# Attention weights turned by VectorE and regrouped by transfers, and fp32 scores with heads side by side, from the second batch on

## The chip, the cores and the metric

The kernel runs on one NeuronCore of a Trainium2 chip. The metric is the device time of one execution in microseconds, lower is better. The engines of the core that matter here are TensorE (PE in the profile, with its weight loads as PEld), VectorE (DVE), ScalarE (ACT), GpSimd (POOL), and SyncE (SP), which issues every DMA.

## What is computed

Block-causal attention over 8 batches of 8 heads, 576 tokens, 64 channels per head, followed by a gated MLP with a spatial gate. All inputs are float32.

```python
# attention, block = 64
scores = scale * np.matmul(q, k.transpose(0, 1, 3, 2))
scores = np.where(block_i >= block_j, scores, -1000000000.0)
attn = np.exp(scores - np.max(scores, axis=-1, keepdims=True))
attn = attn / (np.sum(attn, axis=-1, keepdims=True) + 1e-09)
x = heads_side_by_side(np.matmul(attn, v))          # (8, 576, 512)
# gated MLP
h = np.maximum(x @ w_in, 0.0)                       # (8, 576, 1024)
u, v = (h[..., :512], h[..., 512:])
v_n = (v - mean(v)) / np.sqrt(var(v) + 1e-06)
v_s = np.einsum('ts,bsd->btd', w_spatial, v_n) + b_spatial[None, :, None]
return (u * v_s) @ w_out
```

## The kernel before, in words

Batches are numbered 0 to 7 here. Heads go in pairs, four pairs a batch (`NPAIR`), the first head of a pair in partitions 0 to 63, the second in 64 to 127. A pair has nine score tiles (`TILES`): for each head the query tiles t = 0 to 3 with 128, 256, 384 and 512 keys, and one tile for query block 8 of both heads, with all 576 keys. The main loop at L639 walks over all tiles of all pairs, one tile a step.

A step calls `scores` (L276). PE forms the tile, DVE copies it from PSUM with the mask and takes the row minimum of the scaled negative (L298, L319), ACT takes the exponential with the row sum (L325), DVE forms the reciprocal (L331, L334), and POOL multiplies it in (L338). In batch 0 the products take the float32 operands (L293). From batch 1 on the operands are split into an upper and a lower part in the rounded type fp32r: ACT rounds (L222), DVE and POOL subtract (L225), ten transfers a pair stack the parts so that two products over 128 rows give all cross terms (L235 to L243, L296, L297; three for the tile of block 8, L315).

Some steps later `transposes` (L353) turns the tile with PE through an identity, in 128 by 128 pieces (L366 to L388), into PSUM, and ACT or DVE copies the result to SBUF (L369, L376, L383). `av_lo` (L408) and `av_hi` (L422) multiply with the values in float32, the two heads in the two column halves of the array, and `x_evac` splits the output into two parts (L404 and L405). The last 64 tokens are copied once more, both parts side by side, by POOL into `xs` (L445).

`moe` (L451) returns 29 groups of matmuls for a batch: five `v_group` (the normalised half; 12 matmuls of 512 columns, the one for the last 64 tokens 8), eight `u_group`, eight `sp_group` (the spatial gate, 14 matmuls of 288 columns), eight `out_group` (12 of 288). All use fp32r parts in three products. The groups of batch b run during the steps of batch b + 1, 29 groups for 36 steps, so that one group stands between about any two attention tiles. A group's PSUM bank comes from a pool of two (`ps_m`, tag `m`). A v group's chain runs on ACT (relu, L473), DVE (statistics L489 and L490, small ops L493 to L505), ACT (L491, L492), and DVE (L509, L516, L517). The output tile `o` has two buffers, and each goes out by a DMA on SP (L588).

The order on each engine is fixed when the program is built: a scheduler places the instructions of the written order, with some freedom where nothing depends.

## Time and profile before

| what | value |
|---|---|
| runs | 761.75, 763.27, 765.53 us (median 763.27) |
| span of the profiled execution, first to last instruction | 760.0 us |
| the profiled execution's own time beside its span | the page gives the span alone; the median of the runs is 3.3 us above it |
| PE busy | 750.3 us, 5284 matmuls |
| DVE, ACT, POOL busy | 486.7, 453.3, 316.7 us |
| DMA moved | 96.37 MB, 52% busy share of the 16 engines in batches 1 to 7 |
| granted TensorE clock | 1.00 in every stretch asked for |

A matmul's record has a start and a modelled end, and neighbours overlap in the pipeline. So the time that a matmul takes from PE is read from start to start, or from the chain of waits, which gives each piece the time by which it moves the chain on, and not from its recorded length. A float32 product appears as two records (two passes), an fp32r product as one. Times within a batch are given from the first v group of one batch to the same place of the next.

### The profile page before, as it was taken

The page shows a single profiled execution, that of the slowest core. Times are in us where ns is not written, and L with a number is a line of the kernel's source. Part 1 is how long each engine was busy: PE and PEld are TensorE (multiplying, and loading weights), DVE is VectorE, ACT ScalarE, POOL GpSimd, SP SyncE. Part 2 cuts the span into 40 slices and gives each one's busy share as a digit, 9 for nine tenths or more (in the row PEclk, how much of TensorE's full clock was granted, in tenths as well). Part 3 has the DMA queues.
Part 4 walks back from the last instruction along what each step waited for, and adds up shares of the span by engine and source line. Part 5 has one row for each costly group of instructions (what it writes and reads, how often), then busy time and mean ns, then how long its engine had stood idle before and what let it go on. Part 6 is the DMA issues. An engine that isn't in the chain of part 4 may idle for free.

```text
span 760.0 us, 16034 instructions
## 1 busy us (share of the span) xinstructions
PE 750.3 (99%) x5284; PEld 648.9 (85%) x5284; DVE 486.7 (64%) x1744; ACT 453.3 (60%) x1236; POOL 316.7 (42%) x478
## 2 busy tenths in 40 slices
PE   8999899999999999999999999999999999999998
PEld 5567798988888889988888889988889988888898
DVE  6997985668545785448755487555865568543641
ACT  6786766655665656566656566655666556654232
POOL 4785775423444325443344334433344423423011
DMA  6477585555465445464355554456454554430001
GB/s 216 138 212 219 146 232 128 129 134 124 114 171 125 115 119 135 133 173 111 85 141 150 141 124 103 127 152 159 106 130 116 139 146 112 92 77 33 0 9 55
DMA packets 43814, 96.37 MB, mean 127 GB/s; under 512 B 6866, under 2 KB 15570, under 8 KB 43732
## 3 DMA queue, kind: packets, MB, share of 16 engines
q1 hardware_dynamic: 43732, 95.35, 48.4%
q8 instruction: 42, 0.69, 0.4%
q14 instruction: 40, 0.33, 0.1%
HBM read 38.18 MB, written 9.44 MB: 63 GB/s over the span
## 4 chain that ended last, share of the span: by engine, by line
PE 87%; DVE 7%; ACT 2%; issue 2%; DMA 1%; SPq 0%; DVEq 0%; ACTq 0%
PE mo L581 14%; PE ms L560 13%; PE mu L537 12%; PE mv L468 11%; PE avh L430 7%; PE t L375 6%; PE s L297 4%; PE s L296 4%; PE s L315 3%; PE avl L415 3%; PE t L382 2%; PE t L368 2%; PE mv L479 1%; PE avh L434 1%; DVE p L298 1%
## 5 line engine op out<-in xcount | busy, mean ns | idle before, releaser
L338 POOL TENSOR_SCALAR p<-p,ssum 128x384 f32<-128x384 f32 (+4 forms) x288 | 175.0, 615 | 252.0 <-DVE ssum L334 96.6
L325 ACT ACTIVATE p<-p,nmax 128x384 f32<-128x384 f32 (+4 forms) x288 | 168.5, 586 | 59.4 <-DVE nmax L298 38.7
L298 DVE CUSTOM_DVE_ANT_0 p<-s,mask 128x128 f32<-128x128 f32 (+3 forms) x256 | 122.7, 486 | 60.2 <-PE s L297 46.4
L537 PE MATMUL mu<-x,wi_hi 128*128 128x288 f32 x512 | 116.3, 303 | 0.5 <-DVE vr L485 0.5
L537 PEld LDWEIGHTS mu<-x,wi_hi 128*128 128x128 f32 x512 | 85.4, 188 | 2.9 <-ACT pthi L376 1.0
L468 PE MATMUL mv<-wi_hi,x 128*128 128x512 f32 x256 | 85.9, 396 | 0.0
L225 POOL TENSOR_TENSOR lo<-raw,hi 128x288 fp32r<-128x288 f32 (+1 forms) x83 | 68.3, 837 | 37.4 <-ACT hi L222 37.4
L331 DVE TENSOR_SCALAR ssum<-ssum 128x1 f32<-128x1 f32 (+1 forms) x224 | 39.1, 175 | 63.8 <-ACT p L325 63.3
L560 PE MATMUL ms<-ws_hi,vh 128*128 128x288 f32 x256 | 78.6, 307 | 0.0
L560 PE MATMUL ms<-ws_hi,vl 128*128 128x288 f32 x256 | 75.4, 294 | 0.0
L560 PE MATMUL ms<-ws_lo,vh 128*128 128x288 f32 x256 | 75.3, 294 | 0.0
L581 PE MATMUL mo<-gh,wo_hi 128*128 128x288 f32 x256 | 74.5, 314 | 0.5 <-ACT gh L568 0.5
L376 ACT COPY pthi<-t 128x384 f32<-128x384 f32 (+1 forms) x128 | 67.8, 530 | 9.9 <-PE t L375 9.1
L568 ACT CAST gh<-u 128x288 fp32r<-128x288 f32 x64 | 27.7, 433 | 75.1 <-DVE u L567 72.7
L297 PE MATMUL s<-st 128*128 128x128 f32 (+1 forms) x224 | 72.3, 323 | 0.0
L296 PE MATMUL s<-st 128*128 128x128 f32 (+1 forms) x224 | 71.5, 321 | 0.0
L375 PE MATMUL t<-ident,p 128*128 128x128 f32 x448 | 70.8, 275 | 0.4 <-POOL p L338 0.3
L537 PE MATMUL mu<-x,wi_lo 128*128 128x288 f32 x256 | 69.7, 295 | 0.0
L581 PE MATMUL mo<-gh,wo_lo 128*128 128x288 f32 x256 | 69.7, 295 | 0.0
L569 POOL TENSOR_TENSOR gl<-u,gh 128x288 fp32r<-128x288 f32 x48 | 38.7, 806 | 64.6 <-ACT gh L568 63.8
L430 PE MATMUL avh<-pthi,v 128*64 128x320 f32 x384 | 61.0, 441 | 0.4 <-DVE x L405 0.4
L375 PEld LDWEIGHTS t<-ident,p 128*128 128x128 f32 x448 | 52.3, 141 | 8.6 <-issue 3.0
(119 smaller groups left out, 1726.0 us busy)
## 6 DMA issues: line engine op xcount, KB each, us to landing
raw<-qk SPq DMA_DIRECT2D x31, 608.0 KB, 5.0
st<-lo SPq DMA_DIRECT2D x112, 144.0 KB, 3.1
st<-hi SPq DMA_DIRECT2D x56, 272.0 KB, 3.2
v<-v SPq DMA_DIRECT2D x32, 320.0 KB, 3.4
outT<-o SPq DMA_DIRECT2D x64, 144.0 KB, 2.5
st<-hi SPq DMA_DIRECT2D x56, 144.0 KB, 3.1
st<-lo SPq DMA_DIRECT2D x56, 128.0 KB, 3.3
rwi<-w_in SPq DMA_DIRECT2D x8, 512.0 KB, 4.5
```

Source lines behind the costliest of these rows:

```text
L225: (nc.vector if n < (2 if (b, pr) == (1, 0) else 1) else nc.gpsimd).tensor_tensor(out=lo[:, cs], in0=raw[:, cs], in1=hi[:, cs].bitcast(F32 ...
L296: nc.tensor.matmul(ps[:, :n], st[:, qs], st[:, Q8:Q8 + n], start=True, stop=False)
L297: nc.tensor.matmul(ps[:, :n], st[:, qs], st[:, :n], start=False, stop=True)
L298: nc.vector.tensor_tensor_reduce(out=pt[:, :n], in0=ps[:, :n], in1=mask[:, 512 - n:], scale=-0.125, scalar=BIG, op0=ALU.add, op1=ALU.min, ...
L325: nc.scalar.activation(pt[:, :n], pt[:, :n], AF.Exp, bias=mx, scale=-1.0, accum_out=ssum[:, sc:sc + 1])
L338: nc.gpsimd.tensor_scalar(out=pk[:, :nk], in0=pk[:, :nk], scalar1=ssum[:, 2 + sc - k:3 + sc - k], scalar2=1.0, op0=ALU.mult, op1=ALU.mult,)
L375: nc.tensor.transpose(bk[:, c, :], pt[:, c * P:(c + 1) * P], ident)
L430: nc.tensor.matmul(av[js, 0:320], vt[:, c, js], hi[:, j, c, :], start=(c == 0), stop=False)
L468: nc.tensor.matmul(ps, xs[k][:, j, cs], w[:, k, DH:], start=(n == 0), stop=(n == 3 * NC - 1),)
L537: nc.tensor.matmul(ps[:, :HT], w[:, k, ds], xs[k][:, j, zs], start=(n == 0), stop=(n == 3 * NC - 1),)
L560: nc.tensor.matmul(ps[:, :HT], a[:, ds], w[:, k, zs], start=(n == 0), stop=False)
L581: nc.tensor.matmul(ps[:, :HT], w[:, k, es], a[:, k, :], start=(n == 0), stop=(n == 3 * ND - 1),)
```

## The change

In batch 0 the attention stays as it was (its output columns are stored in another token order, so one copy becomes two). From batch 1 on:

- **Scores** take the float32 operands from the raw tile. The splitting (`prep_pair`, its ACT, DVE and POOL instructions and its transfers) is gone. A pair's eight tiles t = 3 to 0 are written as one run, the two heads alternating, each in its own 64 rows of the array; the tile of block 8 stands ahead of it (`scores_8`, `scores_run`).
- **Transposes** leave PE. `turn_blocks` turns the tile on DVE in 32 by 32 blocks (`nc.vector.transpose`, 13 instructions a pair, 3,200 elements a partition) into one tile `pb`, and `regroup` issues four transfers a head on SP, which gather the blocks into `ptt`. Tokens are stored in another order (`tokens`), and the inputs and the output are permuted to it on the host. The PSUM copies of the transposes on ACT and DVE are gone.
- **Outputs** of a pair are one run of 20 products (`av_pair`), placed right behind the scores of the next pair.
- **MLP**: PE's order is now fixed as written (`mm`). One group stands between the block-8 tile and the score run, and the others behind the outputs, as many as a credit in microseconds allows. The group of the last 64 tokens comes first in its batch instead of fifth. In a v group the scaling and the rounding move from DVE to ACT, the subtraction from DVE to POOL; in the last sp group of four the subtraction moves to POOL.
- Score, output and transpose banks are used as one ring of six (`RING`).

```diff
-    raw_p = ctx.enter_context(tc.tile_pool(name="raw_p", bufs=1))
-    hl_p = ctx.enter_context(tc.tile_pool(name="hl_p", bufs=1))
-    qk_p = ctx.enter_context(tc.tile_pool(name="qk_p", bufs=3))
+    raw_p = ctx.enter_context(tc.tile_pool(name="raw_p", bufs=2))
...
-    p_p = ctx.enter_context(tc.tile_pool(name="p_p", bufs=4))
+    p_p = ctx.enter_context(tc.tile_pool(name="p_p", bufs=6))
...
-    def prep_pair(b, pr):
...
+    def mm(out, lhsT, rhs, start, stop):
+        ins = nc.tensor.matmul(out, lhsT, rhs, start=start, stop=stop).ins
+        if last[0] is not None:
+            tc.add_manual_dep(
...
+    RING = [(ps_s, "s")] * 3 + [(ps_t, "t")] * 2 + [(ps_av, "av")]
...
+    def scores_8(b, pr):
...
+        for z in range(2):
+            ps = bank(f"s8_{b}_{pr}_{z}")
+            mm(ps[:, :HT], raw[:, Q8:], raw[:, z * HT:(z + 1) * HT], True, True)
...
+    def scores_run(b, pr):
...
+        for t in (3, 2, 1, 0):
+            for hd in range(2):
...
+                mm(ps[(t, hd)], raw[js, S + t * P:S + (t + 1) * P], raw[js, :n], True, True)
+        for ts in ((3,), (2,), (1, 0)):
...
+                    soft(st, t, hd, p[:, at:at + n], [ps[(t, hd)]])
...
+            normalise(st, tiles)
...
+    def turn_blocks(b, pr, t, hd):
...
+        if t == 8:
+            dims = [[XH, 8], [1, 16]]
+            nc.vector.transpose(to(P, [[P, 3], *dims]), p8[:, :384])
+            nc.vector.transpose(to(304, dims), p8[:, 384:512])
+            nc.vector.transpose(to(144, dims), p8[:, 512:640])
+            return
...
+        nc.vector.transpose(to(hd * XH + 32 * t, [[P, m], *dims] if m > 1 else dims), p[:, :m * P])
+        if t == 3:
+            nc.vector.transpose(to(hd * XH + x_at(3, 3), dims), p[:, 3 * P:])
+
+    def regroup(b, pr, hd):
...
+        for a in range(4):
+            nc.sync.dma_start(ptts[(b, pr)][:, a, xs], pb[32 * a:32 * a + 32, :, xs])
...
+    def av_pair(b, pr):
...
+        for z in range(2):
+            av = bank(f"av_{b}_{pr}_{z}")
...
+            for c in range(5):
+                for j in range(2):
...
+                    mm(
+                        to[js, :, PA - C_N[c]:], vt[:, c, js],
+                        ptt[:, 2 * z:2 * z + 2, at:at + C_N[c]], c == 0, c == 4,
+                    )
...
-            nc.vector.tensor_scalar(
-                out=vr[:m, :], in0=vr[:m, :], scalar1=st[:m, 12:13], scalar2=st[:m, 13:14],
-                op0=ALU.mult, op1=ALU.add,
+            nc.scalar.activation(
+                vr[:m, :], vr[:m, :], AF.Identity, bias=st[:m, 13:14], scale=st[:m, 12:13]
             )
...
-                nc.vector.tensor_copy(vh, vr)
-                nc.vector.tensor_tensor(
+                nc.scalar.copy(vh, vr)
+                nc.gpsimd.tensor_tensor(
...
-            (nc.vector if dc == ND - 1 else nc.gpsimd).tensor_tensor(
+            nc.gpsimd.tensor_tensor(
...
+        vs = [(G_V if c < FULL else G_VT, lambda c=c: v_group(c)) for c in (FULL, 0, 1, 2, 3)]
...
+    for g in range(NPAIR, len(pairs)):
+        b, pr = pairs[g]
+        credit += G_PAIR
...
+        scores_8(b, pr)
+        group()
+        scores_run(b, pr)
+        if g > NPAIR:
+            av_pair(*pairs[g - 1])
+            if pr == 0:
+                queue += moe(b - 1)
...
+        while group():
...
+            for f in rest[:3]:
+                f()
+            del rest[:3]
+        for f in rest:
+            f()
```

Here `C_N` is (144, 112, 80, 48, 16), `rest` holds the pair's block-8 turn, its tile turns and its two regroups, and `normalise` issues POOL's multiplication per tile, as L338 did.

Three places show what the new order is. The first is PE's stream where a batch ends and the first MLP group that needs it begins. Names are output<-weights and moving operand: `avh` and `av` are attention outputs, `mv` a v group, `x` an output of a pair, `xs` its last 64 tokens. Before:

```order
L430 MATMUL avh_3_3563<-pthi_3_3225,v_3_2815 64x320 x6
L434 MATMUL avh_3_3563<-pthi_3_3225,v_3_2815 64x192 x2
L439 MATMUL avh_3_3563<-ptc_2_3_3226,v_3_2815 64x64 x2
L296 MATMUL s_0_4_3580<-st_0_1_3183 128x256
L297 MATMUL s_0_4_3580<-st_0_1_3183 128x256
L468 MATMUL mv_0_3589<-wi_hi,x_0_2451 128x512
L468 MATMUL mv_0_3589<-wi_lo,x_0_2451 128x512
```

and now:

```order
L231 MATMUL av_3_1_1946<-ptt_3_1793,v_3_1490 64x2x80 x2
L231 MATMUL av_3_1_1946<-ptt_3_1793,v_3_1490 64x2x48 x2
L231 MATMUL av_3_1_1946<-ptt_3_1793,v_3_1490 64x2x16 x2
L231 MATMUL mv_4_1964<-wi_hi,xs_1189 128x512
L231 MATMUL mv_4_1964<-wi_lo,xs_1189 128x512
```

The first group behind the batch's last outputs was a v group that reads `x`; it is now the group of the last 64 tokens, which reads `xs`, and the scores of a whole pair stand right ahead of the outputs.

The second place is POOL's stream around the write of that `xs`. Before (`p` are tiles of attention weights, `lo` a lower part of the split):

```order
L338 TENSOR_SCALAR p_3_8_3380<-p_3_8_3380,ssum_3_8_3379 128x512
L225 TENSOR_TENSOR lo_1_3470<-raw_1_3437,hi_1_3469 128x288 x2
L338 TENSOR_SCALAR p_0_0_3420<-p_0_0_3420,ssum_0_0_3419 128x576
L225 TENSOR_TENSOR lo_1_3470<-raw_1_3437,hi_1_3469 128x128
L338 TENSOR_SCALAR p_0_1_3463<-p_0_1_3463,ssum_0_1_3462 128x128
L338 TENSOR_SCALAR p_0_2_3495<-p_0_2_3495,ssum_0_1_3462 128x256
L445 TENSOR_SCALAR xs_2452<-x_3_3399 128x128
```

and now (`p_2_0_0` and `p_2_0_1` are the tiles of the next batch's first pair, `p_96` its block-8 tile):

```order
L497 TENSOR_SCALAR p_96<-p_96,sst_0_1871 128x576
L497 TENSOR_SCALAR p_2_0_0_1896<-p_2_0_0_1896,sst_0_1871 128x512
L497 TENSOR_SCALAR p_2_0_1_1899<-p_2_0_1_1899,sst_0_1871 128x512
L497 TENSOR_SCALAR p_2_0_0_1906<-p_2_0_0_1906,sst_0_1871 128x384
L497 TENSOR_SCALAR p_2_0_1_1909<-p_2_0_1_1909,sst_0_1871 128x384
L497 TENSOR_SCALAR p_2_0_0_1916<-p_2_0_0_1916,sst_0_1871 128x256
L497 TENSOR_SCALAR p_2_0_0_1916<-p_2_0_0_1916,sst_0_1871 128x128
L497 TENSOR_SCALAR p_2_0_1_1921<-p_2_0_1_1921,sst_0_1871 128x256
L497 TENSOR_SCALAR p_2_0_1_1921<-p_2_0_1_1921,sst_0_1871 128x128
L409 TENSOR_SCALAR xs_1189<-x_3_1943 128x128
```

All nine tiles of a pair of the next batch are normalised ahead of the copy that the first MLP group reads.

The third place is DVE's stream at the statistics of the last full v group (`st_3`, of `vr_3`). Before:

```order
L517 TENSOR_TENSOR vl_2_2508<-vr_2_2483,vh_2_2507 128x512
L331 TENSOR_SCALAR ssum_1_1_2512<-ssum_1_1_2512 128x2
L334 RECIPROCAL ssum_1_1_2512<-ssum_1_1_2512 128x2
L298 ISA p_1_3_2600,nmax_1_3_2598<-s_1_3_2601,mask 128x128
L298 ISA nmax_1_3_2598 128x1
L489 BN_STATS st_3_2571<-vr_3_2570 128x6
```

and now:

```order
L396 TENSOR_TENSOR x_0_2229<-av_0_0_2218,x_0_2229 128x288
L494 RECIPROCAL sst_1_2143<-sst_1_2143 128x4
L396 TENSOR_TENSOR x_0_2229<-av_0_1_2233,x_0_2229 128x288
L563 STREAM_TRANSPOSE pb_1_2280<-p_2_1_0_2202 128x2x4x32
L563 STREAM_TRANSPOSE pb_1_2280<-p_2_1_0_2202 128x4x32
L563 STREAM_TRANSPOSE pb_1_2280<-p_2_1_1_2207 128x2x4x32
L563 STREAM_TRANSPOSE pb_1_2280<-p_2_1_1_2207 128x4x32
L639 BN_STATS st_3_2253<-vr_3_2252 128x6
```

The statistics now stand behind all thirteen block turns of the pair, the last four of which are shown.

## Prediction

> **What bounds the kernel now.** First the page's busy times and the shares of the chain of work that ended last.

> ```profile
> PE 750.3 (99%) x5284; PEld 648.9 (85%) x5284; DVE 486.7 (64%) x1744; ACT 453.3 (60%) x1236; POOL 316.7 (42%) x478
> PE 87%; DVE 7%; ACT 2%; issue 2%; DMA 1%; SPq 0%; DVEq 0%; ACTq 0%
> ```

> PE is never without a matmul, and it is most of the chain. Next the busy times by stretch, each from the same place of one batch to that of the next (columns: us, PE, PEld, DVE, ACT, POOL, clock, DMA share, GB/s).

> ```profile
> 156.44:247.84 91.40, 91.40 (x661) 80.76 (x661) 58.01 (x213) 55.68 (x153) 36.66 (x58) 1.00 0.52 131
> 430.66:522.07 91.41, 91.41 (x661) 80.77 (x661) 58.03 (x213) 55.71 (x153) 36.66 (x58) 1.00 0.53 133
> ```

> The period is 91.41 us, PE fills all of it, and DVE has 58. Seven such periods (attention of batches 1 to 7 beside the MLP of 0 to 6) are 640 of the 760.0 us; the other 120 are batch 0's attention and the last MLP, which the change leaves nearly alone. So the question is one period: what PE must do in it, and how long PE now waits in it. The chain in order of time (start, us, piece) prices PE's work:

> ```profile
> 301.81 1.57 PE mo L581 x12
> 303.38 0.23 PE s L296
> 303.61 0.23 PE s L297
> 303.84 0.33 PE t L375 x3
> 304.17 0.80 PE avl L415 x8
> 304.97 1.78 PE mo L581 x12
> 306.75 0.79 PE s L315 x6
> 307.54 0.44 PE t L375 x4
> ...
> 313.09 1.77 PE avh L430 x12
> 314.86 0.32 PE avh L434 x4
> 315.18 0.26 PE avh L439 x4
> 315.44 1.79 PE ms L560 x12
> 317.24 0.13 PE ms L564
> 317.37 0.14 PE ms L565
> ...
> 352.71 2.77 PE mv L468 x12
> ```

> A group of 12 matmuls of 288 columns takes 1.57 us, and 1.78 behind float32 work: a change of kind costs about 0.2. MLP of a batch, without such changes: four v groups of 2.77, the short one (8 of 12) 1.85, eight u and eight out groups of 1.57, eight sp groups of 1.57 + 0.27 = 1.84: 11.1 + 1.85 + 25.1 + 14.7 = 52.8 us. The rest of the period, 38.6 us or 9.65 a pair, is attention and changes of kind.

> **The change, PE's part.** What float32 scores cost stands in batch 0's timeline (start, time to the last end):

> ```profile
> 23.41 1.12 PE L293 MATMUL s<-raw 64*128 64x512 f32 x2
> 24.46 0.33 PE L366 MATMUL t<-ident,p 128*128 128x128 f32 x1
> 24.63 0.38 PE L368 MATMUL t<-ident,p 128*128 128x128 f32 x2
> 24.85 1.14 PE L315 MATMUL s<-raw 128*128 128x288 f32 x4
> 25.82 0.27 PE L366 MATMUL t<-ident,p 128*128 128x128 f32 x1
> 27.14 0.70 PE L293 MATMUL s<-raw 64*128 64x256 f32 x2
> 27.76 0.66 PE L375 MATMUL t<-ident,p 128*128 128x128 f32 x4
> 30.05 0.92 PE L293 MATMUL s<-raw 64*128 64x256 f32 x4
> 31.03 0.63 PE L375 MATMUL t<-ident,p 128*128 128x128 f32 x4
> ```

> The block-8 tile takes 24.85 to 25.82, 0.97 us for 4 × 288 columns: 0.84 ns a column and pass. A 512-column tile of one head takes 23.41 to 24.46, 1.05 (0.86 and 0.2 of start). The row with x4 holds a 256- and a 384-column tile of the two heads next to each other: 0.98 us in all, where the 256 alone took 0.62 (27.14 to 27.76) and the 384 by the column price 0.65 + 0.2. So two heads in two row halves do run at once. The run of a pair is then 2 × (512 + 384 + 256 + 128) × 0.84 = 2.15 + 0.25; block 8 is 0.97 + 0.15. Outputs keep their columns: before 0.80 + 1.77 + 0.32 + 0.26 = 3.15 a pair for 1,600 columns in two passes with two starts, now 2.7 + 0.15 with one. Transposes go; their share of the chain in these four batches is in the chain's shares by line (the answer ends where the row ends here):

> ```profile
> by line: PE mu L537 14.4%; PE ms L560 14.3%; PE mo L581 14.3%; PE mv L468 12.1%; PE avh L430 7.7%; PE t L375 6.8%; PE s L297 5.6%; PE s L296 5.3%; PE s L315 3.7%; PE avl L415 3.5%; PE mv L479 2.0%; PE t L382 2.0%; PE t L368 1.9%; PE avh L43
> ```

> 6.8 + 2.0 + 1.9% of 91.4 and two lesser lines are 2.5 us a pair, as eight groups of 0.33 to 0.44 would be less their overlap. With 0.2 for leaving the runs, a pair costs 6.6 us, a batch 26.4. Together 52.8 + 26.4 = 79.2; I take 79.6 for gaps between groups. **PE's work falls from 91.4 to 79.6 us a batch.**

> **The other engines.** The groups by line and shape (busy, mean ns):

> ```profile
> L325 ACT ACTIVATE p<-p,nmax 128x384 f32<-128x384 f32 (+4 forms) x288 | 168.5, 586 | 59.4 <-DVE nmax L298 38.7
> L325 ACT ACTIVATION_READ_ACCUMULATOR p<-p,nmax 128x1 f32 x288 | 54.1, 188 | 0.0
> L338 POOL TENSOR_SCALAR p<-p,ssum 128x384 f32<-128x384 f32 (+4 forms) x288 | 175.0, 615 | 252.0 <-DVE ssum L334 96.6
> L369 DVE COPY ptlo<-t 128x384 f32<-128x384 f32 x56 | 30.5, 545 | 0.0
> L225 DVE TENSOR_TENSOR lo<-raw,hi 128x512 fp32r<-128x512 f32 x28 | 27.1, 967 | 5.0 <-DMA st<-hi 3.9 <-ACT o L587 0.4
> L568 ACT CAST gh<-u 128x288 fp32r<-128x288 f32 x64 | 27.7, 433 | 75.1 <-DVE u L567 72.7 <-DVE fwo L149 2.4
> L569 POOL TENSOR_TENSOR gl<-u,gh 128x288 fp32r<-128x288 f32 x48 | 38.7, 806 | 64.6 <-ACT gh L568 63.8
> ```

> No row shows a block turn on DVE. Bounds: the copy L369, 545 ns for 384 elements, which less its start is about 1.0 ns an element, and L225, 967 for 512, 1.9 an element. The copy has the same size and one operand as a turn has, so it is the nearest; with part of its start hidden behind the neighbour (an estimate) I take 0.46 us for 384 and 0.2 for 128: 4.2 us a pair for 13 turns, 17 a batch, at the upper end 28. [...] DVE gives back the splits (0.97 a pair), the copies of L369 (1.09), and a v group's three full-width instructions. So its 58 us a batch stay near 55, of 80 to 90: room in sum. ACT and POOL stay under 60 and 45. Eight transfers a pair take the place of ten of like size, and the DMA share of 0.52 stays.

> So sums do not bind; **order does**. PE's stream is now fixed, attention comes in one burst a pair, and the burst passes DVE, ACT, POOL, DVE. I follow it with T as the start of the score run. ACT gets the first tile at T + 1.7 and needs 8 × (586 and the half of the 188 ns accumulator read that stands out) = 5.4 us; POOL needs 8 × 0.6 = 4.8 behind pairs of exponentials, and ends at T + 9 to 10; the turns end just behind. Regrouping (issue 0.6 each, as below, landing 3) ends near T + 17, and its reader stands at the next pair's T + 2.4, 20 us on: hidden by 5 us. Four waits are not hidden:

> - **A, start of a batch.** Here score run and block 8 follow each other with no group between, then the outputs (2.85), then `mv_4`, whose seventh matmul needs `xs`: PE is there at T + 2.4 + 2.95 + 1.4 = 6.8. POOL writes `xs` behind all nine normalisations, at T + 10.3. PE waits 3.5 us.
> - **B, last v group.** Its statistics stand behind the turns (T + 10.8); ACT's logarithm behind them, and behind that, in ACT's order, the copy that frees `mu_1_0`'s bank. PE wants the bank at T + 11.1 and gets it at T + 12.3; with a second such wait 1.4 us.
> - **C, sp to out, twice a batch.** Behind the last sp group a DVE product, ACT's 0.43 (L568) and POOL's 0.81 (L569) follow, and DVE comes to it late, behind turns; 1.0 us each.
> - **D, output buffers.** Behind eight regroup issues on SP the first `outT` leaves near T + 14 and lands at T + 17; the third out group's copy waits for its buffer, and the bank with it: 1.4 us.

> ```profile
> 301.20 1.37 SPq L243 DMA_DIRECT2D st<-lo  x2
> ```

> Two issues of this queue take 1.37 us, the 0.65 each that I use. Bounds of the four: nothing, if ACT and POOL run a tile earlier than their means say, and twice as much. **Sum:** 79.6 + 3.5 + 1.4 + 2.0 + 1.4 = 87.9 a batch, 3.5 less than now; 7 × 3.5 = 24.5. The last MLP starts on `xs` and subtracts on POOL: + 1. From 760.0: 736.5. The median of the runs is 3.3 above that span, so **740 us**.

> **Rivals.**

> - **The waits are hidden.** DVE's 55 and ACT's 56 us of 80 speak for it. Without waits the period is 79.6: 760 − 7 × 11.8 + 1 + 3.3 = 682; with half, 711. Chance 0.18.
> - **Turns are slow (ends slower).** At L225's price a pair's turns cost 2.8 us more. 1,900 of the 3,200 elements stand ahead of A's output copy (+ 1.7), all ahead of B's statistics (+ 2.8) and of both C's (+ 5.6): the period becomes 98.0, the time 760 + 7 × 6.6 + 4 = 810. It turns against the kernel from 1.3 of the 1.9 ns. Chance 0.16.
> - **A cold start of PE.** A's wait would be PE's first real pause. At the program's start PE's matmuls of 128 columns come 0.21 us apart (four in 1.06, the last with its 0.42 of length), where batch 0's column price gives 0.107:

> ```profile
> 1.63 1.06 PE L85 MATMUL warm<-mask 128*128 128x128 f32 x4
> ```

>   If a pause of 3.5 us brings that pace back for as long as there, some 2.6 us, it adds 1.3 for each of six batches and lengthens what follows: 748. Chance 0.08; all stretches show a clock of 1.00 so far. [...]
> - **Heads one after the other.** Then 2.15 more a pair: 740 + 28 × 2.15 = 800. The x4 row speaks against it. Chance 0.05.

> **How the numbers follow.** The forecast has 0.53, and with the waits between half and one and a half times my sum spans 711 to 770. A measurement of this kernel can tell about 0.5% from no change, so faster means under 759.5 and slower over 767. Forecast 0.48 faster, 0.04 the same, 0.01 slower; hidden waits 0.18 faster; slow turns 0.13 slower, 0.03 the same; cold start 0.07 and 0.01 slower; heads apart 0.05 slower. Sum: 0.73, 0.07, 0.20. The range 690 to 785 leaves out the end of the first rival (0.06), the worse part of the second (0.09) and the last (0.05).

> **What would show it.** PE's share falls under 95%, with idle rows on `mv` released by POOL `xs`, on `mu` by ACT, on `mo` by POOL or ACT, at the sizes above. The period is 79.6 plus them. A turn of 384 elements under 0.55 us keeps the forecast, one of 0.8 makes it fail upward. Matmuls of two heads that start some ns apart show the halves at once. An output that waits for a transfer would show regrouping late, which I hold hidden. If PE shows no pauses, the first rival is right.

## The result and the profile after

The changed kernel takes 818.74 us (median of four, 817.51 to 821.04) where the kernel before takes 762.51 (761.38 to 765.53): a ratio of 1.073, interval 1.070 to 1.076. It is slower by 56 us. The profiled execution after spans 818.1 us, the one before 760.0.

First the same two rows of the page as before: busy times, and the shares of the chain of work that ended last.

```profile
PE 718.9 (88%) x4864; PEld 609.0 (74%) x4864; DVE 456.6 (56%) x1739; ACT 383.7 (47%) x1088; POOL 288.5 (35%) x444
PE 36%; DVE 25%; ACT 11%; SPq 8%; DMA 8%; POOL 6%; issue 5%; DVEq 0%; POOLq 0%; ACTq 0%
```

PE was 99% busy and 87% of the chain; now it is 88% busy and 36% of the chain, and no other engine is fuller than before. So nothing new is saturated: the chain passes from engine to engine. Next two periods, from a place of one batch to the same of the next (columns as before: us, busy times, granted clock, DMA share, GB/s).

```profile
205.03:304.01 98.98, 86.57 (x601) 74.86 (x601) 55.45 (x215) 44.78 (x129) 32.02 (x52) 0.95 0.45 117
304.01:403.20 99.19, 86.31 (x600) 74.95 (x600) 55.30 (x214) 44.64 (x129) 32.01 (x52) 0.95 0.46 117
```

The period grew from 91.4 to 99.1 us. Two things are to be seen: PE stands still for 12.6 us of it, and the granted clock (the share of PE's full clock that the profile says it was given), which was 1.00 in every stretch of the kernel before, is 0.95. The second is the surprise. Three stretches around one pause show where it comes from:

```profile
369.17:372.58 3.41, 1.09 (x6) 1.00 (x7) 2.54 (x9) 0.32 (x1) 1.89 (x5) 1.00 0.16 20
372.58:375.99 3.41, 3.41 (x14) 3.12 (x13) 2.52 (x8) 1.06 (x4) 0.00 (x0) 0.50 0.87 191
375.99:379.41 3.42, 3.42 (x21) 3.06 (x21) 2.12 (x5) 1.92 (x3) 0.00 (x0) 1.00 0.88 212
```

In a stretch of 3.41 us PE is busy for 1.09. The next 3.41 us run at a granted clock of 0.50, and then it is 1.00 again. PE gets through 14 matmuls in the slow stretch and 21 in the one behind it. The timeline of PE at the same place (start, us, what, idle before it and its releaser):

```profile
371.49 0.50 PE L231 MATMUL mv<-wi_hi,xs 128*128 128x512 f32 x1 [3.76 <-POOL xs L409]
...
374.93 0.63 PE L231 MATMUL mv<-wi_lo,x 128*128 128x512 f32 x1
375.35 0.63 PE L231 MATMUL mv<-wi_hi,x 128*128 128x512 f32 x1
...
376.35 0.39 PE L231 MATMUL mv<-wi_lo,x 128*128 128x512 f32 x1
376.58 0.39 PE L231 MATMUL mv<-wi_hi,x 128*128 128x512 f32 x1
```

From start to start a matmul of 512 columns takes 0.42 us in the slow stretch and 0.23 behind it. PE's waits over the whole run (us in total, times, longest):

```profile
PE mv L231 <- POOL xs L409: 24.4, 7, 4.0
PE ms L231 <- ACT o L736: 19.7, 7, 3.3
PE mo L231 <- DVE u L716: 19.6, 14, 2.4
PE mu L231 <- ACT u L691: 16.7, 7, 2.7
PE mo L231 <- ACT gh L717: 3.4, 15, 0.3
```

In the order of the rows these are the prediction's waits A, D, C, B, and the rest of C: seven times each (C twice a batch), 84 us together. The first of the seven periods differs from the others: its A is 1.6 us and its D 1.2, where the other six have 3.7 to 4.0 and 2.8 to 3.3.

From here on each span is split into three parts: **idle** is the span less PE's busy time; **lost to the clock** is the span times one less the mean granted clock (it counts a slow stretch as half lost, pauses in it too); **work** is what is left. Before: 750.3 work, 9.7 idle, 0 lost. After: 718.9 − 37.6 = 681.3 work, 99.2 idle, and with the clock row below 818.1 × 0.046 = 37.6 lost. So the change did take 69 us of work from PE, and paid 89.5 for pauses and 37.6 for a slower clock: − 69.0 + 89.5 + 37.6 = 58.1, the difference of the two spans.

```profile
core 0: 818.1 us, clock 0.954
```

### The profile page after: what moved, and what is told of

It is laid out like the page before. It is cut to its first block, busy times and chain, and to the rows that moved or that the text cites. A ratio compares the mean times of both kernels' runs of the same rounds, so it can differ in the third digit from the quotient of the medians.

```text
span 818.1 us, 14375 instructions
## 1 busy us (share of the span) xinstructions
PE 718.9 (88%) x4864; PEld 609.0 (74%) x4864; DVE 456.6 (56%) x1739; ACT 383.7 (47%) x1088; POOL 288.5 (35%) x444
## 4 chain that ended last, share of the span: by engine, by line
PE 36%; DVE 25%; ACT 11%; SPq 8%; DMA 8%; POOL 6%; issue 5%; DVEq 0%; POOLq 0%; ACTq 0%
PE mu L231 9%; SPq L574 8%; PE mv L231 8%; DVE pb L563 7%; ACT p L483 7%; DVE p L476 7%; PE ms L231 6%; DMA outT<-o 6%; PE s L231 5%; POOL p L497 5%; PE mo L231 4%; DVE sst L491 2%; DVE pb L556 2%; DVE x L396 2%; ACT vr L659 1%
## 5 line engine op out<-in xcount | busy, mean ns | idle before, releaser
L497 POOL TENSOR_SCALAR p<-p,sst 128x384 f32<-128x384 f32 (+4 forms) x252 | 137.0, 560 | 194.7 <-DVE sst L494 117.9
L483 ACT ACTIVATE p<-p,sst 128x384 f32<-128x384 f32 (+4 forms) x252 | 145.0, 577 | 53.6 <-DVE sst L476 52.4
L476 DVE CUSTOM_DVE_ANT_0 p<-s,mask 128x384 f32<-128x384 f32 (+4 forms) x252 | 114.3, 471 | 58.8 <-PE s L231 58.6
L231 PE MATMUL mu<-x,wi_hi 128*128 128x288 f32 x512 | 126.0, 328 | 17.2 <-ACT u L691 16.7
L231 PE MATMUL s<-raw 64*128 64x256 f32 (+4 forms) x640 | 126.5, 440 | 3.4 <-DVE nmax L291 1.8
L231 PEld LDWEIGHTS mu<-x,wi_hi 128*128 128x128 f32 x512 | 96.7, 215 | 21.2 <-ACT u L691 18.7
L716 DVE TENSOR_TENSOR u<-ms,u 128x288 f32<-128x288 f32 x64 | 28.0, 437 | 148.0 <-PE ms L231 148.0
L231 PEld LDWEIGHTS s<-raw 64*128 64x128 f32 (+1 forms) x640 | 73.2, 188 | 41.9 <-issue 19.8
L563 DVE STREAM_TRANSPOSE pb<-p 128x384 f32<-128x384 f32 (+2 forms) x224 | 98.3, 455 | 8.7 <-POOL p L497 7.0
L231 PE MATMUL ms<-ws_hi,vh 128*128 128x288 f32 x256 | 83.8, 327 | 19.7 <-ACT o L736 19.7
L231 PE MATMUL mo<-gh,wo_hi 128*128 128x288 f32 x256 | 73.7, 308 | 23.0 <-DVE u L716 19.6
L231 PE MATMUL av<-ptt,v 128*64 128x32 f32 (+4 forms) x1120 | 87.7, 306 | 2.8 <-DVE sst L476 2.7
L666 POOL TENSOR_TENSOR vl<-vr,vh 128x512 fp32r<-128x512 f32 x32 | 41.1, 1286 | 134.4 <-ACT vh L665 134.4
L231 PEld LDWEIGHTS av<-ptt,v 128*64 128x64 f32 x1120 | 75.6, 137 | 15.8 <-DVE sst L476 4.8
```

Source lines behind the costliest of these rows:

```text
L231: ins = nc.tensor.matmul(out, lhsT, rhs, start=start, stop=stop).ins
L476: nc.vector.tensor_tensor_reduce(out=p[:, at:at + n], in0=ps, in1=mk, scale=-0.125, scalar=BIG if m == 0 else st[:, k:k + 1], op0=ALU.add, ...
L483: nc.scalar.activation(p, p, AF.Exp, bias=mx, scale=-1.0, accum_out=st[:, 10 + k:11 + k])
L497: nc.gpsimd.tensor_scalar(out=p, in0=p, scalar1=st[:, k:k + 1], scalar2=1.0, op0=ALU.mult, op1=ALU.mult)
L563: nc.vector.transpose(to(hd * XH + 32 * t, [[P, m], *dims] if m > 1 else dims), p[:, :m * P])
L666: nc.gpsimd.tensor_tensor(out=vl, in0=vr, in1=vh.bitcast(F32), op=ALU.subtract)
```

## The experiments

Twelve kernels were run, all made from the changed kernel. "Ratio" is to the kernel before, timed again together with the run.

| run | median us | ratio (interval) | clock | work | idle | lost |
|---|---|---|---|---|---|---|
| changed kernel | 818.74 | 1.073 (1.070 to 1.076) | 0.954 | 681 | 99 | 38 |
| fill_pauses | 808.67 | 1.061 (1.058 to 1.065) | 0.983 | 742 | 55 | 14 |
| fill_two | 802.46 | 1.050 (1.048 to 1.053) | 0.974 | 723 | 57 | 21 |
| o_four | 785.21 | 1.031 (1.026 to 1.035) | 0.964 | 680 | 72 | 28 |
| out_on_act | 795.71 | 1.044 (1.040 to 1.047) | 0.972 | 684 | 81 | 22 |
| stats_later | 820.49 | 1.077 (1.075 to 1.080) | 0.958 | 683 | 99 | 34 |
| copies_first | 800.38 | 1.048 (1.043 to 1.052) | 0.966 | 686 | 86 | 27 |
| outputs_first | 794.66 | 1.043 (1.040 to 1.046) | 0.955 | 679 | 76 | 36 |
| three_fixes | 778.39 | 1.019 (1.016 to 1.023) | 0.960 | 680 | 65 | 31 |
| three_spread | 778.88 | 1.019 (1.016 to 1.022) | 0.965 | 683 | 67 | 27 |
| products_first | 775.05 | 1.015 (1.011 to 1.020) | 0.971 | 689 | 63 | 22 |
| all_edges | 747.51 | 0.980 (0.977 to 0.984) | 0.990 | 688 | 51 | 7 |
| all_edges_four | 814.45 | 1.069 (1.062 to 1.077) | 0.966 | 679 | 103 | 28 |

The three right columns are of the profiled execution, in us; that of `out_on_act` is the fastest of its four and 7.6 us under their median, the others lie within 4 us of theirs. Work is the same in all of them, within 10 us (the two kernels with spare matmuls carry 55 and 41 us of those), so what tells the kernels apart is idle time and clock.

**Is the slow clock a cost of its own?** The first two runs leave the long waits where they are and give PE something to do in them. `wi_hi` is a weight at hand, `ps` the bank that the group is about to overwrite.

```diff
+    def fill(n, ps):
+        for _ in range(n):
+            mm(ps[:, :HT], wi_hi[:, 0, :P], wi_hi[:, 0, :HT], True, True)
...
+                fill(26 if 0 < b < B - 1 else 0, ps)                        # mv_4
...
+            fill(15 if b < B - 1 and (z, dc) == (1, 1) else 0, ps)          # mu_1_1
...
+            fill(22 if b < B - 1 and (z, ec) == (0, 3) else 0, ps)          # mo_0_3
```

> Spare matmuls (26, 15 and 22 of 288 columns, about 0.13 us each) stand in PE's order ahead of the three groups next to the long pauses: 26 ahead of mv_4, 15 ahead of mu_1_1, 22 ahead of mo_0_3. They write a bank that the group then overwrites, so nothing of the result changes and no wait is removed; PE only has work while it waits. Theory 'half clock': behind each of these pauses the trace shows 3.41 us at a granted clock of 0.5, worth about 1.7 us of work; 20 such stretches go, the mean granted clock rises from 0.954 to 0.99, the time falls by about 34 us to 785. Rival 'waits alone': the pauses cost their own length and the records of the clock say nothing of the time: 818, within 4. Rival 'spare work is too long': it delays the copies that free the banks and the time rises over 825.

Measured 808.67: faster by 10 us, not by 34. The clock did what was expected (0.983), so the slow stretches do follow the pauses; but the spare work ahead of `mu_1_1` changed more than PE. PE's waits behind it:

```profile
403.78 0.40 PE L231 MATMUL mu<-x,wi_hi 128*128 128x288 f32 x1 [0.66 <-ACT u L697]
406.49 0.40 PE L231 MATMUL mu<-x,wi_hi 128*128 128x288 f32 x1 [0.85 <-ACT u L697]
```

The second wait is new: as `mu_1_1` ends later, the copy of its bank falls behind another cast in ACT's order. Idle and spare matmuls (415, 0.133 us apart) are 55 + 55 = 110 us together, where the changed kernel was idle for 99: the waits became longer. So the run was repeated without those 15.

> As fill_pauses, but spare matmuls only ahead of mv_4 (26) and mo_0_3 (22), not ahead of mu_1_1. In fill_pauses three half-clock stretches a batch were gone and the period fell by only 3.2 us; 15 spare matmuls ahead of mu_1_1 had moved the copy of its bank behind another cast on ACT, and mu_1_3 waited 0.85 anew. Theory 'half clock, 1.5 us a stretch' (mu and mv behind A took 5.88 before and 4.40 without it): 13 stretches go and no new wait comes: 13 x 1.5 = 20, so 798. Rival 'a stretch is worth 0.3 of its 3.4 us' (3.2 a batch over three): 13 x 1.05 = 14, so 805. Rival 'waits alone': 818.

Measured 802.46, 16.3 less than the changed kernel. The ledger says what it is: lost to the clock fell from 37.6 to 801.3 × 0.026 = 20.8, by 16.8, while idle and spare matmuls (310) are 57 + 41 = 98, the 99 of the changed kernel. The waits are the same and the time is not: **here a slow stretch cost half of its length, on top of the wait ahead of it.** The place of A, now with spare matmuls in the pause:

```profile
361.77 1.35 PE L231 MATMUL mv<-wi_hi 128*128 128x288 f32 x9
...
364.36 0.40 PE L231 MATMUL mv<-wi_hi,xs 128*128 128x512 f32 x1
...
366.71 0.40 PE L231 MATMUL mv<-wi_lo,x 128*128 128x512 f32 x1
366.94 0.40 PE L231 MATMUL mv<-wi_hi,x 128*128 128x512 f32 x1
```

The seventh matmul (364.36) follows without a wait, and the 512-column matmuls of the next group come 0.23 us apart at once. The wait for `xs` itself is untouched; PE is merely kept busy through it. The forecast of 798 counted 13 stretches less; by the time some nine went (16.3 / 1.7, an estimate), so some stayed or came back.

**Wait D: the output buffers.**

```diff
-    o_p = ctx.enter_context(tc.tile_pool(name="o_p", bufs=2))
+    o_p = ctx.enter_context(tc.tile_pool(name="o_p", bufs=4))
```

> Four output buffers in place of two, nothing else. Theory: the wait of ms_1_0 for the copy of an output (19.7 us in seven) comes from the first outT that stands on SP behind regroup issues; with four buffers no copy waits, the pause of 2.8 goes and with it the half-clock stretch behind it: 7 x (2.8 + 1.7) = 31.5, so 787. Rival 'waits alone': 7 x 2.8 = 19.7, so 799. Rival 'the queue binds': the transfers leave as late as before, the next group's copy or a regroup waits in its place, 812 or more.

Measured 785.21, where the theory had 787. The parts agree less well than the sum: idle fell by 27, where 19.7 was priced, and the clock's share by 9.5, where 11.9 was. Wait D went as expected; A fell too, from 24.4 to 18.7, which the theory did not have. In the changed kernel the cause can be read off SP's queue and ACT's timeline at one such place:

```profile
327.61 2.39 SPq L574 DMA_DIRECT2D ptt<-pb  x2
330.10 5.47 SPq L737 DMA_DIRECT2D outT<-o  x4
...
326.74 0.40 ACT L736 COPY o<-mo 128x288 f32<-128x288 f32 x1 [1.37 <-PE mo L231]
328.32 0.40 ACT L736 COPY o<-mo 128x288 f32<-128x288 f32 x1 [1.18 <-PE mo L231]
334.34 0.79 ACT L736 COPY o<-mo 128x288 f32<-128x288 f32 x2 [5.62 <-DMA outT<-o]
```

The first output is copied by 327.1, but its transfer is issued only at 330.10, behind the regroup issues, and the third copy waits 5.62 us for it. To see how much of that is the queue's order and how much the landing, the next run leaves two buffers and only changes who issues.

```diff
-            nc.sync.dma_start(outT[b, es, z * HT:(z + 1) * HT], o)
+            nc.scalar.dma_start(outT[b, es, z * HT:(z + 1) * HT], o)
```

> Still two output buffers, but each outT is issued by ACT right behind its copy, not by SP behind the regroup issues. Theory 'queue order' (step D of the prediction): outT leaves at once, its buffer is back after a landing of 2 to 4 us, the copy of the third group waits at most 1 us instead of 5.6, and the pause of ms_1_0 goes with its half-clock stretch, as in o_four: 785 to 790. Rival 'landing': the transfers themselves take as long, whoever issues them, and 2 us or more of the pause stay: 800 or more. Rival 'issue on ACT': issuing costs ACT 0.6 us each ahead of its copies, and the waits at mo and mu grow: 810 or more.

Measured 795.71, between the theory and the rival. PE's wait at this place is

```profile
PE ms L231 <- ACT o L736: 6.3, 7, 1.5
```

against 19.7 before: 13.4 of the 19.7 us go with the place in SP's queue, and 6.3 stay while the copies wait for landings, for which two buffers are too few (27 copies now wait for a transfer, at most 4.2 us). An issue took ACT 0.34 to 0.39 us in four at one such place, where the third rival had 0.6.

**Wait B: the copy behind the logarithm.** ACT and DVE in the changed kernel, just before PE's pause at `mu_1_2`:

```profile
398.02 0.59 ACT L623 ACTIVATE vr<-mv 128x512 f32<-128x512 f32 x1
402.55 0.29 ACT L641 ACTIVATE st<-st,eps 128x1 f32<-128x1 f32 x1 [3.94 <-DVE st L640]
402.75 0.39 ACT L691 ACTIVATE u<-mu 128x288 f32<-128x288 f32 x1
...
400.27 1.46 DVE L563 STREAM_TRANSPOSE pb<-p 128x256 f32<-128x256 f32 x4 [0.34 <-POOL p L497]
401.65 0.65 DVE L639 BATCH_NORM_STATS2 st<-vr 128x6 f32<-128x512 f32 x1
```

The logarithm waits 3.94 us for statistics that stand behind turns, and the copy of `mu_1_0` (402.75), which needs nothing of it, stands behind the logarithm. The first try moved the statistics chain in the written order (here cut to its core):

```diff
+            late.append(lambda: v_rest(c, m, vr, st))
...
             nc.scalar.activation(u_tile()[:, dc, zs], ps[:, :HT], AF.Relu)
+            while late:
+                late.pop(0)()
```

> The statistics chain of a v group is written behind the copy of the next u group instead of ahead of it, so ACT's logarithm no longer stands ahead of the copy that frees mu_1_0's bank. Theory: the wait of mu_1_2 for ACT (16.7 us in seven) and the half-clock stretch behind it go: 7 x (2.4 + 1.7) = 28.7, so 790. Rival 'waits alone': 802. Rival 'the chain is late': vh and vl of the last group come later than the first sp group needs them, and a wait there takes the place: 815 or more.

Measured 820.49: no change, and the profile says why. At this place ACT's order is the same as before (in the whole run six of its 1,088 instructions moved, and none on DVE):

```profile
400.15 0.29 ACT L648 ACTIVATE st<-st,eps 128x1 f32<-128x1 f32 x1 [3.99 <-DVE st L647]
400.36 0.39 ACT L698 ACTIVATE u<-mu 128x288 f32<-128x288 f32 x1
```

So the scheduler put the logarithm back ahead, whatever the written order. The run tells nothing about B. The next one adds an order edge.

```diff
+            held["u"] = nc.scalar.activation(u_tile()[:, dc, zs], ps[:, :HT], AF.Relu).ins.name
...
-            nc.scalar.activation(st[:m, 8:9], st[:m, 7:8], AF.Ln, bias=eps[:m, :])
+            e = nc.scalar.activation(st[:m, 8:9], st[:m, 7:8], AF.Ln, bias=eps[:m, :])
+            behind(e, "u")
```

`behind(e, key)` adds a dependency without a semaphore, as `mm` does: `e` comes later on its engine than the instruction kept under `key`. The chain of the last full group is written behind two copies.

> stats_later changed the written order, but ACT's order in the program stayed: the logarithm still stood ahead of the copies. Here an order edge puts the logarithm of the last full group behind the copies of mu_1_0 and mu_1_1 (and that of the other groups behind the next copy). Theory: the pause at mu_1_2 (2.4) goes with its half-clock stretch (1.5); as the scaling now stands ahead of the copy of mu_1_2, ms_0_0 waits about 1.3: 7 x (2.4 + 1.5 - 1.3) = 18, so 800. Rival 'it only moves': ms_0_0 waits for the bank or for vl as long as mu_1_2 did: 815 or more. Rival 'statistics bind': vl comes so late that the time rises over 822.

Measured 800.38, where the theory had 800, and with the new wait that it named:

```profile
PE ms L231 <- ACT u L710: 6.9, 6, 1.4
```

B itself fell from 16.7 to 1.3 us. That the sum fits so closely is partly luck: D fell as well, from 19.7 to 14.1, which the theory did not have.

**Wait A: outputs behind all exponentials.** The copies of the outputs are written between the middle and the small tiles, and edges hold the small tiles' exponentials (ACT) and normalisations (POOL) behind the copies and `xs`.

```diff
+        held["ACT"] = nc.scalar.copy(hi, av).ins.name
...
+        held["POOL"] = nc.gpsimd.tensor_scalar(out=tails[b][:, pr], ...
...
+        if t < 2:
+            behind(e, "ACT")        # e: the exponential in soft
...
+            if t < 2:
+                behind(e, "POOL")   # e: the product in normalise
```

> ACT's copies of a pair's outputs stand ahead of the four exponentials of the two small tiles, and POOL's xs ahead of their normalisations. Theory: xs comes about 2.3 us earlier, the pause at mv_4 falls from 3.5 to about 1.3 in six batches, and a pause that short leaves no half-clock stretch: 6 x (2.2 + 1.7) = 23, so 795. Rival 'waits alone': 805. Rival 'it moves on': the small tiles are turned later, statistics, products and regrouping behind them come later, and the waits at mu, mo or the outputs grow by as much: 815 or more.

Measured 794.66, the number that was expected, but not by the way that was expected. The pause at `mv_4` fell from 24.4 to 14.4 us in seven, wait D vanished, and the waits inside `mo` grew from 23.0 to 27.4; the clock stayed at 0.955. The gain is all idle time (99 to 76); lost to the clock is 36 where it was 38, so the slow stretches stayed, with pauses of up to 2.2 us in front of `mo` (27.4 us in 16 waits for ACT's cast).

**All together.** Four buffers, `copies_first` and `outputs_first`:

> Four output buffers, outputs first on ACT and POOL, copies first: the waits A, B and D together. Theory: the gains add where they are different waits; outputs_first had already taken the wait of D, so its 24 us and the 33 us of o_four share about 7 x 2.8: 818.7 - 33.5 - 24 - 18 + 20 = 763. Rival 'full sum' (the pauses are independent, and with none over 2 us no half-clock stretch is left): 741 or less. Rival 'the waits at mo take the place': with earlier outputs DVE and ACT reach the last products later (27 us in outputs_first), and nothing falls below 780.

Measured 778.39. The sum with D counted once (763) was too good, and the third rival (not below 780) came nearest. The place that is left:

```profile
428.41 1.25 DVE L581 STREAM_TRANSPOSE pb<-p 128x256 f32<-128x256 f32 x3 [0.68 <-POOL p L511]
429.58 0.42 DVE L745 TENSOR_TENSOR u<-ms,u 128x288 f32<-128x288 f32 x1
430.04 0.43 ACT L746 CAST gh<-u 128x288 fp32r<-128x288 f32 x1 [2.12 <-DVE u L745]
430.52 0.61 PE L231 MATMUL mo<-gh,wo_hi 128*128 128x288 f32 x1 [1.89 <-ACT gh L746]
430.93 0.44 PE L231 MATMUL mo<-gh,wo_lo 128*128 128x288 f32 x1
```

This is wait C as the prediction described it: the gate product (L745) stands behind turns on DVE that themselves wait for POOL, ACT waits for the product, PE for ACT. The 0.44 in the last row, where the mean of this matmul is 0.297 in the changed kernel, is the slow clock again (0.44 as well in the changed kernel's slow stretch, at 372.82): a pause of 1.89 us has been enough here.

The next run changes how many turns and regroups are written behind each MLP group (`rest[:3]` to `rest[:2]`).

> three_fixes with two of a pair's turns and regroups written behind each MLP group in place of three, so that fewer turns stand ahead of the products that mo waits for. Theory: the two waits a batch at mo (C) fall from about 1.9 to 1 us each: 7 x 2 x 0.9 = 13 less than three_fixes. Rival 'the scheduler sets the turns by readiness': no difference over 4 us. Rival 'regrouping late': the turns end later, the transfers land behind their reader, an output waits for ptt and the time is above three_fixes by 5 or more.

Measured 778.88, no difference, and the first rival holds: behind the first period (from 126 us on) DVE's instructions stand in the same order as in `three_fixes`. Fewer turns ahead of the products were thus not tried by this run; it shows only that their written place does not decide. Then edges on DVE:

```diff
+            held["sp"] = nc.vector.tensor_tensor(out=uz, in0=ps[:, :HT], in1=uz, op=ALU.mult).ins.name
...
-        nc.vector.transpose(to(hd * XH + 32 * t, ...
+        e = nc.vector.transpose(to(hd * XH + 32 * t, ...
+        behind(e, "sp" if t < 2 else "DVE")
```

`products_first` has the edge for t < 2 alone; in `all_edges` the turns of the large tiles stand also behind the outputs' lower parts, kept under "DVE" in `x_evac`.

> three_fixes with one more order edge: the turns of the small tiles (t = 0 and 1) stand behind DVE's newest gate product, so that the last product of four, for which ACT and then mo wait, is not queued behind turns that themselves wait for POOL. Theory: the wait inside mo (1.9 us, twice a batch) falls under 0.5 and the half-clock stretch behind each goes: 14 x (1.5 + 1.5) = 42, so 736. Rival 'waits alone': 14 x 1.5 = 21, so 757. Rival 'regrouping late': the small tiles are turned later, ptt lands behind its reader, outputs wait for the transfer, 770 or more.

Measured 775.05, where 736 was expected. The edge moved 14 instructions on DVE, two a period, and the wait for the cast went: so it was the order on DVE that made C. But the group then waits for the lower part on POOL (18.4 us in 28 waits, up to 1.2), `mv_4` waits 16.4 instead of 12.9, and the clock is still 0.971.

> products_first, and the turns of the large tiles (t = 2 and 3) behind DVE's lower parts of the outputs, so that xs comes earlier. Theory: mv_4's wait of 1.9 us falls by 0.9 to 1.7 in six batches: 5 to 10 us less than products_first. Rival 'xs is not bound by DVE': no difference over 3. Rival 'regrouping late': as the period shortens, the transfers of a pair land behind their reader and the outputs wait for ptt: no gain, or up to 10 lost.

Measured 747.51: faster than the kernel before, by 2.0% (ratio 0.980, interval 0.977 to 0.984, so between 1.6 and 2.3%), and 27.5 below `products_first` where 5 to 10 were expected. One period and the main waits:

```profile
339.74:426.50 86.76, 82.25 (x604) 70.86 (x601) 54.18 (x213) 45.27 (x129) 31.90 (x53) 1.00 0.52 135
...
PE mo L231 <- POOL gl L752: 11.3, 27, 0.5
PE mv L231 <- POOL xs L421: 8.9, 7, 1.6
```

The clock is 1.00 through the period. Idle time is 12 us shorter than in `products_first`, and 15 more come from the clock (22.5 to 7.5 lost): it is 1.00 from 252.60 to 426.50 us and from 513.50 to 600.00, where `products_first` has 0.95 over a period (346.80 to 440.00). So more than half of this step is clock, which the expectation had left out. The pauses of the earlier runs were shortened without that gain, as long as some of them still ended in slow stretches, and this is one reason why sums of single gains were wrong both ways.

The last run halves the number of regroup transfers.

```diff
-        xs = slice(hd * XH, (hd + 1) * XH)
+        if not hd:
+            return
+        xs = slice(0, 2 * XH)
```

> all_edges with four regroup transfers a pair, each with both heads, in place of eight of one head. Theory: SP needs half the issues (0.8 each, 6.4 us a pair now), the regroup of a pair starts about 2 us later and ends about 1 us sooner: within 5 of all_edges if nothing waits for ptt, and 5 to 10 better if outputs wait there. Rival 'size sets the issue': four issues take as long as eight, the first half starts later, and the time is 5 or more above.

Measured 814.45, worse than the rival put it. First the page's row of the regroup transfers (issues, KB each, median us from the start of an issue to landing), in `all_edges` and here, then SP's queue, DVE's turns and PE's waits here:

```profile
ptt<-pb SPq DMA_DIRECT2D x224, 200.0 KB, 4.0
ptt<-pb SPq DMA_DIRECT2D x112, 400.0 KB, 6.5
...
420.43 0.55 SPq L597 DMA_DIRECT2D ptt<-pb  x1
...
426.85 1.51 SPq L597 DMA_DIRECT2D ptt<-pb  x2
...
434.86 0.58 DVE L574 STREAM_TRANSPOSE pb<-p 128x384 f32<-128x384 f32 x1 [2.91 <-DMA ptt<-pb]
...
PE av L231 <- DVE sst L488: 34.7, 15, 3.4
PE av L231 <- DMA ptt<-pb: 29.3, 8, 4.3
```

The turns of this pair are done at 420.4 and the first transfer leaves at once, but the last two leave at 426.85, since on SP the transfers now stand in turn with `outT`. That alone does not make them late: the last issue ends at 428.36, 3.0 us ahead of the next score run (431.38), and in `all_edges` one pair's ended 3.1 us ahead of it (399.25 and 402.35). What has grown is the landing, from 4.0 to 6.5. The next pair's first turn waits 2.91 us for it (`pb` has one buffer), and DVE's copies of the scores stand behind that turn; for the banks that these free, PE's outputs wait 34.7 us in all, besides the 29.3 for the transfers themselves. Nor is much saved on the issues: ten of them take SP 14.0 us around this place (399.67 to 452.64), 5.6 for four, where sixteen of `all_edges` took 13.7 (390.56 to 421.51), 6.9 for eight, so the rival's premise holds in large part. How much of the longer landing is the size and how much the company of `outT`, no run takes apart.

## Why the prediction was wrong

Forecast: a period of 87.9 us and 740 in all, at 0.73 for faster. Measured: 99.1 and 818.74, slower. In the three parts from above the forecast for the profiled execution was 668 work (7 × 79.6, and 110 in the rest of the span), 69 idle (7 × 8.3, the 9.7 of before, and 1) and 0 lost; measured were 681, 99 and 38. The error of 82 us is 13.6 of work, 30.4 of waits and 37.6 of clock.

- **The step that failed: the cold start, taken as a rival of 0.08.** The prediction had it as a cost of A alone, 1.3 us in six batches, because "all stretches show a clock of 1.00 so far". But those rows came from a kernel whose longest pause of PE was 1.6 us, and could not speak of longer ones. So the sum had no term for the clock. Measured it is 37.6 us: in the last six of the seven periods each of A, B and D is met by a stretch of 3.41 us at half clock or two, 1.7 us each, 5.1 a period, while the two pauses of 1.3 us at C are not. `fill_two` shows this cost by itself: the time fell by 16.3 us and what is lost to the clock by 16.8. At A (372.58) PE was busy for 1.09 of the 3.41 us ahead of the slow stretch. With a forecast of five pauses of 1 to 3.5 us in each period, an estimate of this cost belonged into the sum, not among the rivals.
- **Waits, right in kind, short in size.** All four came where the prediction put them, released by what it named. A was 3.5 forecast and 24.4 / 7 = 3.5 measured, 3.8 without the short first one. B was 1.4 and is 16.7 / 7 = 2.4; C was 2.0 and is (19.6 + 3.4) / 7 = 3.3; D was 1.4 and is 19.7 / 7 = 2.8. Together 8.3 forecast and 12.0 measured. For D, in the pair whose score run starts at T = 313.43, the first `outT` was issued at T + 16.7 and the third copy began at T + 20.9, where T + 14 and T + 17 were forecast: eight regroup issues take 6.95 us, 0.87 each and not 0.65, and the landing takes 4.1 and not 3. For B (T = 389.28) the statistics began at T + 12.4 and not at T + 10.8, because POOL ended at T + 12.1, where T + 9 to 10 was forecast; its last normalisations waited for a reciprocal that stands on DVE behind turns and lower parts, which the sum had left out:

```profile
399.76 1.62 POOL L497 TENSOR_SCALAR p<-p,sst 128x256 f32<-128x256 f32 x4 [1.27 <-DVE sst L494]
```

- **PE's work: nearly right.** 79.6 forecast; measured 82.2 in a period of `all_edges` at full clock. The gain was 9.2 a period instead of 11.8. Heads in two row halves do run at once: the sixteen records of a pair's score run take 2.43 us, where 2.4 was forecast, so the rival of one after the other is out.
- **Turns: right.** The groups by shape after:

```profile
L563 DVE STREAM_TRANSPOSE pb<-p 128x384 f32<-128x384 f32 x112 | 61.5, 554 | 1.1 <-POOL p L497 0.3
L565 DVE STREAM_TRANSPOSE pb<-p 128x128 f32<-128x128 f32 x56 | 15.1, 269 | 0.0
```

  A turn of 384 elements takes 554 ns by its record, as the copy of the same size did (545), and 0.47 us to the start of the next instruction where nothing waits (369.31 to 369.78), where 0.46 was forecast, not the 730 or more of the slow rival; DVE is at 55.4 a period where 55 was forecast. That the result lies near the 810 of that rival is chance: its mechanism is absent.
- **Regrouping hidden: true, by less.** No output waited for a transfer. But the issues of one pair end late:

```profile
350.78 6.96 SPq L574 DMA_DIRECT2D ptt<-pb  x8
...
362.47 1.22 PE L231 MATMUL av<-ptt,v 128*64 128x288 f32 x10
...
ptt<-pb SPq DMA_DIRECT2D x224, 200.0 KB, 4.1
```

  The last of the eight issues starts at 357.1. With the median of 4.1 from the start of an issue to landing (an estimate for this one) the data are there at 361.2, 1.3 us before the reader, where 5 us were forecast. `all_edges_four` shows what it costs when that margin is gone.
- **Hidden waits (the first rival, 682 to 711)** never came: even `all_edges` keeps 4.5 us of pauses a period.
- **From span to median:** 3.3 us were added; the profiled execution after took 1.9 more than its span (819.96 and 818.1), so this term was 1.4 too large.

Not settled: whether the remaining pauses in `all_edges` can be closed (its list of waits names POOL's lower parts and `xs`), and why `three_fixes` gained less idle time than its parts; no run takes these apart.

## What to carry to other kernels

When a change turns a full engine into one that waits, price each wait twice: by its length, and by what the engine's clock does behind it (here 99.2 us idle and 37.6 lost to the clock); the profile before, with no pause over 1.6 us, said nothing about the second. Before moving work onto engines with room in sum, write down for each in-order queue what will stand behind the new work and who waits for that: here a copy behind a logarithm, a product behind turns and an output behind regroup issues cost 8.5 us a period. Edges that let the awaited instruction go first, and two more output buffers, recovered most of it. A new written order without an edge, in `stats_later` and `three_spread`, did nothing.
